# A LayerNorm-MLP mixer kernel: epsilon inside the statistics aggregation, a new order of loads, and a new order of steps

## The chip, the cores and the metric

The kernel runs on one core of a Trainium2 chip. The metric is device time in microseconds (us). A core has five engines that run side by side: TensorE (PE, matrix products), VectorE (DVE), ScalarE (ACT), GpSimd (POOL) and SyncE (SP), which here only issues DMAs. Engines wait for each other through semaphores.

## What is computed

```
B, S, D, F = 1, 2048, 512, 1792          # bfloat16
h  = gelu(layernorm(x) @ w1)
# four column blocks of h, shifted along S by 1, -1, 2, -2
g0 = shift(h[:, :, 0:128],  +1); g1 = shift(h[:, :, 128:256], -1)
g2 = shift(h[:, :, 256:384], +2); g3 = shift(h[:, :, 384:512], -2)
x1 = x + concat(g0, g1, g2, g3) @ w2
out = x1 + gelu(layernorm(x1) @ w3) @ w4
```

layernorm subtracts the mean over D and divides by sqrt(variance + 1e-5); there is no gain and no bias.

## The kernel before

The 2048 rows are 16 tiles of 128. Each tile passes through the two layers; q numbers the normalisations: q = t in layer 1 and q = 16 + t in layer 2. All of x, of the weights and of the intermediate results stays in SBUF.

For a tile, `ln(layer, t)` records the statistics and the normalisation. On DVE the statistics are bn_stats (L420) and bn_aggr (L422), which leave mean and variance in `mv`; then `vpe` (L427, on DVE or, by the table `VPE`, on POOL) adds epsilon, and POOL computes `rstd` (L438) as vpe to the power of -1/2. For the q in `STAT_ACT` the sums come from two ACT passes instead (L390 for the sum in layer 1, L395 for the squares), with three small DVE instructions behind them (L399 mean, L402, L406). The normalisation `norm` runs on DVE (L459), ACT (L468) or POOL (L471), by the table `NORM`; for the last two a small `nmr` (L464) goes ahead.

The normalised tile must be transposed to `xnT`. For seven tiles PE does it (the steps `sa`/`sb`, `ty`; L504, with the copy out of PSUM `ev` at L512 on the engine that `EVAC` gives). For the other 25 a DMA transpose issued by SP does it (`tp`, L477).

PE's steps stand in a list, `SCRIPT`, and PE runs them in that order: `warm` (L701, matmuls of zeros), `ra`/`rb` and `up1:0`, `up1:1` (tiles 0 and 1 in rows, L542, with gelu at L561 and a transpose `th` at L579, copied out at L585, `evh`), `up1:g` (group g of layer 1, L608, gelu at L623 to `hT`), `mix:t` (tile t times w2, L648, added to x by `x1` at L655 or L659), `up2:g` (group g of layer 2, L608, gelu at L623 to `h2T`), and `down:t` (L677, added and stored at L685 and L688). `GROUPS` says how many tiles each group has.

The loads stand in a second list, `LOADS`. `x7-8` is one DMA of two tiles, `w4a` is half of w4 (896 KB), `@act` puts a load on ACT's queue and all others go to SP. A `tp16` in this list holds a place: the loads behind it are issued only after that transpose has been issued. Names of tiles that PE transposes are skipped there.

All other order is made when the program is built. `order()` gives each instruction a latest start: it counts back from the PE steps through all edges, the edges of the load line among them. `place()` then runs a list schedule with rough durations and writes each engine's order; loads always go first as soon as their line allows it. On the chip each engine runs its own list in order.

```
LOADS = """
x0 w1a w1b x5 tp0 x4 x3 tp5 w2a w2b x7-8 x6 x1@act x11 w3 tp1 x14-15 tp16 x9 x13 x2@act x12 x10 w4b tp2 tp5
tp8 w4a
"""
```

Of the kernel before, what the change touches and what calls it, by code (L numbers as in the profile page):

```python
# [6 lines left out]
P = 128  # L7
ACT_F = mybir.ActivationFunctionType
ALU = mybir.AluOpType
# [16 lines left out]
class Program:  # L26
# [5 lines left out]
    DUE = 191823.0  # L32
    BEGIN = {"sp": 30.0, "act": 150.0, "pe": 400.0, "dve": 150.0, "pool": 450.0}
    ENTRY = 1900.0
    LAG = {"load": 150, "tp": 700}
# [114 lines left out]
    def place(self, succs, order_only):  # L150
# [9 lines left out]
        clock = moved = self.total = 0.0  # L160
# [35 lines left out]
        def land(op):  # L196
            nonlocal moved
            if op.queue == "tp":
                at = max(clock + 500.0, op.start + 2450.0) + self.LAG["tp"]
            elif op.name.startswith("out"):  # L200
                at = clock + 300.0
                self.total = max(self.total, at)
            else:
                moved += op.dur
                at = clock + 650.0 + min(450.0, 0.25 * moved) + (1200.0 if op.dur > 1400.0 else 0.0) + self.LAG["load"]
            for j in succs[op.idx]:
                if (op.idx, j) not in order_only:
                    release(op, self.ops[j], at + 30.0)

        while len(out) < len(self.ops):  # L210
# [18 lines left out]
            if op.queue:  # L229
                tp = op.queue == "tp"  # L230
                free[e] = start + (1300.0 if tp else 460.0)
                rings[e].append([start + (1400.0 if tp else 1000.0), 600.0 if tp else op.dur, op])
                for j in succs[op.idx]:
                    if (op.idx, j) in order_only:
                        release(op, self.ops[j], None)
            else:
                free[e] = start + op.dur
                for j in succs[op.idx]:
                    o = self.ops[j]
                    hop = self.HOP[e] if o.eng != e else (0.0 if e == "pe" else 120.0)  # L240
                    release(op, o, None if (op.idx, j) in order_only else start + op.dur + hop)
# [5 lines left out]
GROUPS = {1: (1, 1, 1, 1, 1, 1, 2, 4, 2, 1, 1), 2: (2, 2, 4, 4, 4)}  # L247
NORM = {5: "pool", 8: "pool", 9: "pool", 10: "act", 11: "pool", 13: "act", 15: "pool", 22: "pool", 23: "act", 26: "pool", 27: "act", 29: "act", 30: "pool"}
EVAC = {2: "dve", 4: "dve", 6: "both", 8: "both", 9: "dve", 10: "both", 11: "both", 13: "dve", 14: "dve", 16: "dve", 17: "both", 18: "dve", 19: "dve", 20: "both", 21: "both", 23: "both", 24: "dve", 25: "dve", 26: "dve", 27: "dve", 28: "dve", 29: "both", 30: "dve"}
SQRT = ()  # L250
STAT_ACT = (1, 7, 8, 11, 18, 19, 20, 21, 25, 26, 27, 28)
HALF = ()
TAIL = (256, 128, 128)
VPE = {0: "pool", 1: "pool", 2: "pool", 3: "pool", 6: "pool", 7: "pool", 8: "pool", 9: "pool", 12: "pool", 14: "pool", 15: "pool", 17: "pool", 19: "pool", 21: "pool", 24: "pool", 25: "pool", 26: "pool", 28: "pool", 29: "pool", 30: "pool", 31: "pool"}
NMR = {0: "pool", 1: "pool", 3: "pool", 4: "pool", 5: "pool", 6: "pool", 8: "pool", 11: "pool", 12: "pool", 13: "pool", 18: "pool", 19: "pool", 20: "pool", 22: "pool", 24: "pool", 26: "pool", 27: "pool"}
NAT = (0, 1)
SPLIT = (0,)
HEV = {3: "dve", 6: "dve"}
BIAS = {"bnag14": -1183, "bnag2": 166.078, "bnag9": -1516, "bnst18": -801.25, "nmr19": 740, "nmr7": 262.923, "nmr9": 377, "norm21": 198.168, "norm31": 61, "ssq0": -1049, "ssq14": -444, "sum17": -602, "tp19": 63, "tp9": 722.116, "vpe7": -589, "vpe8": 45, "x1_3": -682}
LOADS = """  # L260
x0 w1a w1b x5 tp0 x4 x3 tp5 w2a w2b x7-8 x6 x1@act x11 w3 tp1 x14-15 tp16 x9 x13 x2@act x12 x10 w4b tp2 tp5
tp8 w4a
"""
SCRIPT = """
warm:8 sa:0 sb:0 ty:1 ra:0 rb:0 up1:1 th:0 ty:2 th:1 up1:2 mix:0 ty:3 mix:1 ty:4 up1:3 ty:5 up1:4 mix:2
up1:5 mix:3 ty:17 mix:4 up2:0 up1:6 up2:1 mix:6 mix:5 up1:7 down:3 mix:9 up1:8 mix:7-8 up1:9 mix:10-11
up1:10 mix:13 down:0 mix:14 up2:2 down:1 mix:15 up2:3 mix:12 down:7 down:2 down:5 down:11 down:6 up2:4
down:9 down:4 down:8 down:13 down:10 down:12 down:14-15
"""

def bass_standalone__mixer_s_mlp__prompt_kernel(nc, x, w1, w2, w3, w4, out):
# [14 lines left out]
    with ExitStack() as es:  # L286
# [13 lines left out]
        st6 = sb("st6", [P, 2 * NT, 6], F32)  # L300
# [4 lines left out]
        sdv = sb("sdv", [P, 2 * NT], F32)  # L305
        sums = sb("sums", [P, 2 * NT, 2], F32)
        st6b = sb("st6b", [P, len(HALF) + 1, 2, 6], F32)
# [30 lines left out]
        def consts():  # L338
# [5 lines left out]
                   reads=[(("ident",), 0)], writes=[(("ident",), 1)], dur=300)  # L344
            pg.add("pool", "epsc", lambda e: e.memset(eps_c[:], LN_EPS), writes=[(("eps",), 0)], dur=70)
# [6 lines left out]
        def load(item):  # L352
            name, _, eng = item.partition("@")
            eng = eng or "sp"
            if name[0] == "x":
                a, _, b = name[1:].partition("-")
                t0, t1 = int(a), int(b or a) + 1
                if t0 in HALF:
                    for hh, e2 in ((0, "sp"), (1, "act")):
                        cs = slice(hh * D // 2, (hh + 1) * D // 2)  # L360
                        yield pg.add(e2, f"dma_x{t0}_{hh}",
                                     (lambda c: (lambda e: e.dma_start(x_sb[:, t0, c], xt[:, t0, c])))(cs),
                                     writes=[(("x", t0, hh), 0)], dur=190.0, queue=e2)
                else:
                    yield pg.add(eng, f"dma_x{t0}",
                                 lambda e: e.dma_start(x_sb[:, t0:t1, :], xt[:, t0:t1, :]),
                                 writes=[(("x", t, hh), 0) for t in range(t0, t1) for hh in (0, 1)],
                                 dur=(t1 - t0) * 430.0, queue=eng)
            else:
# [7 lines left out]
                             dur=(c1 - c0) * P * src.shape[1] * 2 / (300.0 if src.shape[1] == D else 380.0), queue=eng)  # L377
# [3 lines left out]
        def ln(layer, t):  # L381
            q = t if layer == 1 else NT + t
            src = x_sb[:, t, :] if layer == 1 else x1_sb[:, t, :]
            rs = [(("x", t, 0), 0), (("x", t, 1), 0)] if layer == 1 else [(("x1", t), 0)]
            col = lambda a: a[:, q : q + 1]
            if q in STAT_ACT:
                if layer == 1:
                    b, v = next_junk()
                    pg.add("act", f"sum{q}",
                           (lambda d: (lambda e: e.activation(d, src, ACT_F.Copy, accum_out=sums[:, q, 0:1])))(  # L390
                               junk[:, b, :]),
                           reads=rs, writes=[(("sum", q), 0), (("junk", b), v)], dur=610)
# [5 lines left out]
                pg.add("dve", f"mean{q}",  # L398
                       lambda e: e.tensor_scalar(mv[:, q, 0:1], sums[:, q, 0:1], 1.0 / D, None, ALU.mult),  # L399
                       reads=[(("sum", q), 0)], writes=[(("mv", q), 0)], dur=75)  # L400
# [8 lines left out]
            else:  # L409
                if layer == 1 and t in HALF:  # L410
                    k = HALF.index(t)
                    for hh in (0, 1):
                        pg.add("dve", f"bnst{q}_{hh}",
                               (lambda hh: (lambda e: e.bn_stats(st6b[:, k, hh, :],
                                                                 src[:, hh * D // 2 : (hh + 1) * D // 2])))(hh),
                               reads=[rs[hh]], writes=[(("st6", q, hh), 0)], dur=335)
                    pg.add("dve", f"bnag{q}", lambda e: e.bn_aggr(mv[:, q, :], st6b[:, k, :, :]),
                           reads=[(("st6", q, 0), 0), (("st6", q, 1), 0)], writes=[(("mv", q), 0)], dur=90)
                else:
                    pg.add("dve", f"bnst{q}", lambda e: e.bn_stats(st6[:, q, :], src),  # L420
                           reads=rs, writes=[(("st6", q), 0)], dur=605)
                    pg.add("dve", f"bnag{q}", lambda e: e.bn_aggr(mv[:, q, :], st6[:, q, :]),  # L422
                           reads=[(("st6", q), 0)], writes=[(("mv", q), 0)], dur=75)
                if q not in SQRT:
                    eng = VPE.get(q, "dve")
                    pg.add(eng, f"vpe{q}",
                           lambda e: e.tensor_scalar(col(vpe), mv[:, q, 1:2], LN_EPS, None, ALU.add),  # L427
                           reads=[(("mv", q), 0)], writes=[(("vpe", q), 0)], dur=70 if eng == "dve" else 240)
            if q in SQRT:
                assert q not in STAT_ACT  # L430
                pg.add("act", f"sqrt{q}",
                       lambda e: e.activation(col(sdv), mv[:, q, 1:2], ACT_F.Sqrt, bias=eps_c[:], scale=1.0),
                       reads=[(("mv", q), 0), (("eps",), 0), (("warm",), 0)], writes=[(("sdv", q), 0)], dur=190)
                pg.add("dve", f"rcp{q}", lambda e: e.reciprocal(col(rstd), col(sdv)),
                       reads=[(("sdv", q), 0)], writes=[(("rstd", q), 0)], dur=75)
            else:
                pg.add("pool", f"rstd{q}",
                       lambda e: e.tensor_tensor(col(rstd), col(vpe), neghalf[:], ALU.pow),  # L438
# [416 lines left out]
```

## Time and profile before

| what | value |
|---|---|
| median of 8 runs | 137.28 us (136.88 to 140.02) |
| the profiled execution | 137.3 us, span 136.0 us |
| PE busy | 131.9 us (97% of the span) |
| ACT, DVE, POOL busy | 56.7, 53.0, 29.5 us |
| granted TensorE clock | 1.00 |
| bytes read and written in HBM | 6.82 and 2.10 MB |

The span is the time between the first and the last recorded instruction; the remaining 1.3 us lie around it. In the lines of the profile, "L608" is a line of the kernel file, "y_ps<-xnT,w_sb" says which buffers an instruction writes and reads, "x72" counts merged instructions, and times are us from the start of the span. A line of waits reads: who waited, for whom, us in total, times, longest. A line of the timeline reads: start, duration, engine, line, operation. "DMA to landing" is the time from a DMA's issue to the arrival of its last byte.

### The profile page before, as it was taken

Reading aid. Unit: us, or ns where it says so; the run is one execution under the profiler, and the core shown is the slowest. Engines: PE = TensorE matmul, PEld = TensorE weight load, DVE = VectorE, ACT = ScalarE, POOL = GpSimd, SP = SyncE. Lnnn points to the kernel's source line nnn. Section 1 sums busy time; section 2 is a strip of 40 time slices with the busy share of each in tenths; the row PEclk is TensorE's granted clock in tenths of the full one; section 3 lists DMA queues with packets and bytes.
Section 4 is the critical chain, followed back from the end, with each engine's and each line's share of the span. In section 5 each row is a group of like instructions: output and inputs, shape, how many; then the busy total and the mean of one; then the engine's idle time right before and its main releaser. Section 6 shows DMA issues by size and latency. Waiting matters only on the chain.

```text
span 136.0 us, 2039 instructions
## 1 busy us (share of the span) xinstructions
PE 131.9 (97%) x792; PEld 71.4 (53%) x792; DVE 53.0 (39%) x155; ACT 56.7 (42%) x88; POOL 29.5 (22%) x70
## 2 busy tenths in 40 slices
PE   8999999699999999999999999999999999999994
PEld 3468687687446654444444444444444444444463
DVE  3879989850715796400061003323200002232222
ACT  6589966676433372655406665000055540000000
POOL 2636449990230119500002001000000000000000
DMA  6999589999622003451011000311110001111112
GB/s 210 321 366 389 79 226 268 167 290 119 128 52 64 5 0 77 89 104 39 5 39 38 0 0 0 77 39 43 39 39 0 0 0 39 39 43 39 39 39 77
DMA packets 21913, 12.32 MB, mean 91 GB/s; under 512 B 14480, under 2 KB 21392, under 8 KB 21904
## 3 DMA queue, kind: packets, MB, share of 16 engines
q1 hardware_dynamic: 21184, 11.80, 35.7%
q10 hardware_dynamic: 720, 0.39, 1.0%
q8 instruction: 6, 0.10, 0.3%
q14 instruction: 3, 0.02, 0.1%
HBM read 6.82 MB, written 2.10 MB: 66 GB/s over the span
## 4 chain that ended last, share of the span: by engine, by line
PE 91%; DMA 4%; DVE 2%; ACT 1%; POOL 0%; issue 0%; POOLq 0%; ACTq 0%
PE y_ps L608 40%; PE o_ps L677 36%; PE o_ps L648 10%; DMA xnT<-xn_buf 4%; PE o_ps L701 3%; PE y_ps L542 2%; PE y_ps L504 1%; ACT hn L561 1%; DVE xn_buf L459 0%; DVE x_sb L655 0%; POOL rstd L438 0%; PE o_ps L579 0%; DVE o_sb L685 0%; DVE xnT L512 0%; DVE mv L402 0%
## 5 line engine op out<-in xcount | busy, mean ns | idle before, releaser
L608 PE MATMUL y_ps<-xnT,w_sb 128*128 128x512 bf16 (+2 forms) x424 | 62.9, 307 | 1.3 <-DMA xnT<-xn_buf 1.3
L608 PEld LDWEIGHTS y_ps<-xnT,w_sb 128*128 128x128 bf16 x424 | 37.7, 98 | 26.2 <-ACT h2T L623 1.6
L677 PE MATMUL o_ps<-w_sb,h2T 128*128 128x512 bf16 (+2 forms) x252 | 49.2, 355 | 0.0
L623 ACT ACTIVATE h2T<-y_ps 128x1024 bf16<-128x1024 f32 (+1 forms) x29 | 28.6, 994 | 37.6 <-PE y_ps L608 37.6
L677 PEld LDWEIGHTS o_ps<-w_sb,h2T 128*128 128x128 bf16 x252 | 23.5, 98 | 25.2
L685 DVE TENSOR_TENSOR o_sb<-o_ps,x_sb 128x512 bf16<-128x512 f32 (+2 forms) x18 | 11.4, 632 | 55.5 <-PE o_ps L677 55.5
L438 POOL TENSOR_TENSOR rstd<-vpe,neghalf 128x1 f32<-128x1 f32 x32 | 17.9, 566 | 32.1 <-DVE vpe L406 21.8
L648 PE MATMUL o_ps<-w_sb,hT 128*128 128x512 bf16 x64 | 15.9, 379 | 0.0
L420 DVE BATCH_NORM_STATS2 st<-x_sb 128x6 f32<-128x512 bf16 x20 | 13.6, 681 | 2.3 <-DMA x_sb<-in_x_dram 2.1
L395 ACT ACTIVATE junk<-x_sb 128x512 bf16<-128x512 bf16 x12 | 7.5, 624 | 7.0 <-DVE x_sb L655 7.0
L623 ACT ACTIVATE hT<-y_ps 128x512 bf16<-128x512 f32 (+1 forms) x10 | 7.7, 766 | 4.6 <-PE y_ps L608 4.6
L655 DVE SCALAR_TENSOR_TENSOR x_sb<-o_ps,x_sb 128x512 bf16<-128x512 f32 x8 | 5.5, 686 | 10.4 <-PE o_ps L648 10.3
L459 DVE TENSOR_SCALAR xn_buf<-x_sb,mv,rstd 128x512 bf16<-128x512 bf16 x17 | 7.7, 457 | 4.3 <-POOL rstd L438 4.1
L648 PEld LDWEIGHTS o_ps<-w_sb,hT 128*128 128x128 bf16 x64 | 6.0, 98 | 5.5
L427 POOL TENSOR_SCALAR vpe<-mv 128x1 f32<-128x1 f32 x13 | 3.0, 245 | 21.5 <-DVE mv L422 20.3
L659 DVE TENSOR_TENSOR x_sb<-o_ps,x_sb 128x512 bf16<-128x512 f32 x8 | 5.5, 684 | 4.5 <-PE o_ps L648 4.5
L471 POOL TENSOR_SCALAR xn_buf<-x_sb,rstd,nmr 128x512 bf16<-128x512 bf16 x8 | 6.1, 766 | 0.6 <-DVE nmr L464 0.4
L468 ACT ACTIVATE xn_buf<-x_sb,nmr,rstd 128x512 bf16<-128x512 bf16 x5 | 4.0, 808 | 2.3 <-POOL nmr L464 2.0
L701 PE MATMUL o_ps<-zeros 128*128 128x512 bf16 x8 | 3.6, 631 | 0.6 <-POOLq L840 0.6
L422 DVE BATCH_NORM_AGGREGATE mv<-st 128x2 f32<-128x6 f32 x20 | 3.6, 178 | 0.4
L504 PEld LDWEIGHTS y_ps<-ident,xn_buf 128*128 128x128 bf16 x28 | 2.4, 113 | 1.3 <-DVE mv L399 0.3
L512 ACT ACTIVATE xnT<-y_ps 128x256 bf16<-128x256 bf16 (+1 forms) x6 | 2.8, 485 | 0.5 <-PE y_ps L504 0.5
(34 smaller groups left out, 32.4 us busy)
## 6 DMA issues: line engine op xcount, KB each, us to landing
out_dram<-o_sb SPq DMA_DIRECT2D x15, 128.0 KB, 1.7
w_sb<-in_w_dram SPq DMA_DIRECT2D x1, 1792.0 KB, 9.0
w_sb<-in_w_dram SPq DMA_DIRECT2D x2, 896.0 KB, 5.6
x_sb<-in_x_dram SPq DMA_DIRECT2D x10, 128.0 KB, 3.3
w_sb<-in_w_dram SPq DMA_DIRECT2D x4, 256.0 KB, 4.1
x_sb<-in_x_dram SPq DMA_DIRECT2D x2, 256.0 KB, 6.9
xnT<-xn_buf SPq DMA_TRANSPOSE x25, 2.5
x_sb<-in_x_dram ACTq DMA_DIRECT2D x2, 128.0 KB, 2.9
```

The costliest lines, as they stand in the source:

```text
L395: (lambda d: (lambda e: e.activation(d, src, ACT_F.Square, accum_out=sums[:, q, 1:2])))(junk[:, b, :]),
L420: pg.add("dve", f"bnst{q}", lambda e: e.bn_stats(st6[:, q, :], src), reads=rs, writes=[(("st6", q), 0)], dur=605)
L438: lambda e: e.tensor_tensor(col(rstd), col(vpe), neghalf[:], ALU.pow),
L459: lambda e: e.tensor_scalar(dst, src, mv[:, q, 0:1], rstd[:, q : q + 1], ALU.subtract, ALU.mult),
L471: f = lambda e: e.tensor_scalar(dst, src, rstd[:, q : q + 1], nmr[:, q : q + 1], ALU.mult, ALU.add)
L608: ins = e.matmul(y_ps[:, p, W * i : W * (i + 1)], wsb[:, dc, P * fc : P * (fc + 1)], src[:, dc, P * t0 : P * t0 + W], start=(dc == 0), sto ...
L623: (lambda d, s: (lambda e: e.activation(d, s, ACT_F.Gelu_apprx_tanh)))(dst, ysrc),
L648: ins = e.matmul(dst, hT[:, j, c0 : c0 + P], w2_sb[:, j, :], start=(j == 0), stop=(j == DC - 1))
L655: f = lambda e: e.scalar_tensor_tensor(x1_sb[:, t, :], dst, 1.0, x_sb[:, t, :], ALU.mult, ALU.add, accum_out=sums[:, NT + t, 0:1])
L677: ins = e.matmul(dst, h2T[:, fc, P * t : P * (t + 1)], w4_sb[:, fc, cs], start=(fc == 0), stop=(fc == FC - 1))
L685: (lambda d, c: (lambda e: e.tensor_tensor(o_sb[:, oi, c], d, x1_sb[:, t, c], ALU.add)))(dst, cs),
L701: ins = e.matmul(o_ps[:, b, :], zeros[:, 0:P], zeros[:], start=True, stop=True)
```

## The change

Epsilon: the statistics buffer has nine numbers for each tile instead of six. The last three are a third triple (0, 0, 512 x epsilon), set once by two memsets on POOL. bn_aggr over all three triples gives a variance that already holds epsilon, so `vpe` goes for the tiles whose statistics DVE computes. In layer 1 the ACT pass scales its sum by 1/512 and writes the mean itself. Branches that no tile used (`SQRT`, `HALF`) go.

Loads: the list begins with one run of loads without a transpose between them. w3 comes in halves. w4a and x10 stand behind tp16, w4b behind tp11, and x12-14 and x15 behind tp9.

Order: the rough durations in `place()` are changed (a transpose lands no sooner than 600 ns after the last load, the first PE steps are taken slower, a load behind another DMA costs 800 ns), and the tables and the script are new. `BIAS`, which shifted single instructions, is empty.

```
-            pg.add("dve", f"bnst{q}", lambda e: e.bn_stats(st6[:, q, :], src), ...)
-            pg.add("dve", f"bnag{q}", lambda e: e.bn_aggr(mv[:, q, :], st6[:, q, :]), ...)
-            if q not in SQRT:
-                eng = VPE.get(q, "dve")
-                pg.add(eng, f"vpe{q}", lambda e: e.tensor_scalar(col(vpe), mv[:, q, 1:2], LN_EPS, None, ALU.add), ...)
+            pg.add("dve", f"bnst{q}", lambda e: e.bn_stats(st9[:, q, 0:6], src), ...)
+            pg.add("dve", f"bnag{q}", lambda e: e.bn_aggr(mv[:, q, :], st9[:, q, :]), ...)
+        var = vpe[:, q : q + 1] if q in STAT_ACT else mv[:, q, 1:2]
...
+            pg.add("pool", "trip0", lambda e: e.memset(st9[:, :, 6:8], 0.0), ...)
+            pg.add("pool", "trip1", lambda e: e.memset(st9[:, :, 8:9], D * LN_EPS), ...)
...
-                           ... e.activation(d, src, ACT_F.Copy, accum_out=sums[:, q, 0:1])
+                           ... e.activation(d, src, ACT_F.Copy, scale=1.0 / D, accum_out=mv[:, q, 0:1])
...
-                at = max(clock + 500.0, op.start + 2450.0) + self.LAG["tp"]
+                at = max(clock + 500.0, op.start + 2450.0, last + 600.0) + self.LAG["tp"]
...
-GROUPS = {1: (1, 1, 1, 1, 1, 1, 2, 4, 2, 1, 1), 2: (2, 2, 4, 4, 4)}
-NORM = {5: "pool", 8: "pool", 9: "pool", 10: "act", 11: "pool", 13: "act", 15: "pool", 22: "pool", 23: "act", 26: "pool", 27: "act", 29: "act", 30: "pool"}
-EVAC = {2: "dve", 4: "dve", 6: "both", 8: "both", 9: "dve", ... 17: "both", ...}
-STAT_ACT = (1, 7, 8, 11, 18, 19, 20, 21, 25, 26, 27, 28)
+GROUPS = {1: (1, 1, 1, 1, 1, 1, 2, 2, 2, 2, 2), 2: (2, 2, 4, 4, 4)}
+NORM = {4: "act", 5: "act", 6: "act", 10: "act", 11: "pool", 12: "pool", 13: "act", 15: "act", 18: "pool", 20: "pool", 21: "pool", 22: "pool", 24: "act", 28: "act", 30: "pool"}
+EVAC = {1: "both", 2: "dve", 3: "dve", 7: "both", 9: "dve", ... 17: "both", ...}
+STAT_ACT = (1, 6, 8, 9, 12, 21, 22, 23, 27, 28, 29)
-HEV = {3: "dve", 6: "dve"}
-BIAS = {"bnag14": -1183, "bnag2": 166.078, "bnag9": -1516, ...}
+HEV = {2: "dve", 5: "dve", 6: "dve"}
+BIAS = {}
 LOADS = """
-x0 w1a w1b x5 tp0 x4 x3 tp5 w2a w2b x7-8 x6 x1@act x11 w3 tp1 x14-15 tp16 x9 x13 x2@act x12 x10 w4b tp2 tp5
-tp8 w4a
+x0 w1a w1b x4-5 w2b tp2 x3 w2a x6-7 w3b x8 w3a x1@act x9 x2@act x11 tp16 w4a x10 tp11 w4b tp9 x12-14 x15
 """
 SCRIPT = """
-warm:8 sa:0 sb:0 ty:1 ra:0 rb:0 up1:1 th:0 ty:2 th:1 up1:2 mix:0 ty:3 mix:1 ty:4 up1:3 ty:5 up1:4 mix:2
-up1:5 mix:3 ty:17 mix:4 up2:0 up1:6 up2:1 mix:6 mix:5 up1:7 down:3 mix:9 up1:8 mix:7-8 up1:9 mix:10-11
-up1:10 mix:13 down:0 mix:14 up2:2 down:1 mix:15 up2:3 mix:12 down:7 down:2 down:5 down:11 down:6 up2:4
-down:9 down:4 down:8 down:13 down:10 down:12 down:14-15
+warm:8 sa:0 sb:0 ty:1 ra:0 rb:0 up1:1 ty:2 th:0-1 up1:2 mix:0 ty:4 ty:3 mix:1 up1:3 ty:5 up1:4 mix:2 up1:5
+mix:3 ty:17 mix:4 up2:0 up1:6 up2:1 mix:6 down:1 mix:5 up1:7-8 mix:8 mix:7 up1:9 mix:10 down:0 down:2 mix:9
+up1:10 mix:12 mix:11 up2:2 mix:13 down:3 down:6 mix:14 up2:3 mix:15 down:4-5 down:7 down:11 down:9-10 up2:4
+down:8 down:12 down:14 down:13 down:15
 """
```

## The prediction

> **What bounds the kernel now.** I read the page first, rows 1, 2 and 4, then what PE waits for, then the chain in the window of the one real wait, then SP's order of issue and each transfer's time from issue to landing.
>
> ```profile
> PE 131.9 (97%) x792; PEld 71.4 (53%) x792; DVE 53.0 (39%) x155; ACT 56.7 (42%) x88; POOL 29.5 (22%) x70
> ...
> PE 91%; DMA 4%; DVE 2%; ACT 1%; POOL 0%; issue 0%; POOLq 0%; ACTq 0%
> ...
> PE y_ps L608 <- DMA xnT<-xn_buf: 1.3, 1, 1.3
> PE o_ps L701 <- POOLq L840: 0.6, 1, 0.6
> PE o_ps L579 <- ACT hn L561: 0.2, 1, 0.2
> ```
>
> PE is busy 97% of 136.0 us, and the chain that ended last is PE for 91%. The three lines of waits are everything that PE waits for. So a change can win only these waits, and can lose by opening new ones. The 0.6 is the entry. The 1.3 is one matmul group waiting for a DMA transpose:
>
> ```profile
> 18.75 0.59 POOL rstd L438 x2
> 19.34 5.46 DMA xnT<-xn_buf
> 24.79 0.14 issue
> 24.93 8.02 PE y_ps L608 x72
> ```
>
> The transpose was issued at 19.34 and landed 5.46 us later. SP's timeline around it:
>
> ```profile
> 17.09 0.43 SPq L366 DMA_DIRECT2D x_sb<-in_x_dram  x1
> 17.57 0.43 SPq L374 DMA_DIRECT2D w_sb<-in_w_dram  x1
> 18.05 6.51 SPq L477 DMA_TRANSPOSE xnT<-xn_buf  x5
> 24.60 0.58 SPq L374 DMA_DIRECT2D w_sb<-in_w_dram  x1
> ```
>
> The 17.57 load is w4b (896 KB), directly ahead of the transposes of tiles 6 and 7 that up1:6 needs. Asked one by one, w4b takes 5.4 us to landing (22.97); the first two transposes behind it take 6.3 and 5.5 (24.35 and 24.84). The last fourteen transposes, with no load ahead, take
>
> ```profile
> DMA to landing us min/median/max: 2.4/2.5/2.9
> ```
>
> So a transpose behind a load lands 1.4 to 1.9 us after that load. w4a (issued 24.60, landed 30.5) shows it again: the next transpose lands at 32.4. So does tp16: issued 13.61 behind x14-15 (landed 15.22), it lands at 17.21, 2.0 later.
>
> What the wait costs: up2:0 begins at 17.31 and is 56 matmuls of 256 columns. A group of 16 takes 1.75 in the chain, so 56 take 6.1 and up1:6 could begin at 23.4. It begins at 24.93, so 1.5 us are lost (the page's 1.3 counts from the modelled end).
>
> **The change part by part.**
>
> *PE work.* The script holds the same steps: 8 warm matmuls, seven PE transposes, 64 mix, 252 down and 424 up matmuls. One group of four tiles (3.45) becomes two of two (2 x 1.75); two single tiles (2 x 0.89) become one of two (1.75). +0.05 and -0.03: zero. The tail (down15 in 256, 128, 128) is unchanged.
>
> *Epsilon.* vpe goes from 20 tiles: 13 POOL instructions of 245 ns and 7 DVE of 152 ns. rstd follows bn_aggr directly, which shortens such a tile's chain by 0.2 to 0.3 us. Four means (144 ns of DVE) go as well. The two memsets are like the 98 ns ones on POOL and lie ahead of 3.05, the first bn_aggr: hidden, with over 1 us to spare. bn_aggr over nine numbers instead of six has no row; between 0 and half of its 178 ns more, I take 20 ns, hidden. None of these is on PE's chain except through a transpose that is late anyway for its load. Worth zero alone. If the cover goes (a tile that is just in time), it is worth its 0.25 us.
>
> *Engines of norms and statistics.* norm4, norm5, norm6 go to ACT (808 ns each, L468); ev3 leaves ACT, ev4 comes (592 each); half of ev1 goes to DVE. ACT was busy 8.16 of 8.70 us between 8.6 and 17.3, and DVE 8.17, but on ACT six statistics passes of 0.82 (0.63 and a 0.19 read) fill gaps there and can wait. What must run on ACT between 8.05 and 17.3 afterwards: evh0 and evh1 1.2, norm4 and norm5 1.6, four gelu 2.4, ev4 and ev5 1.2, half of ev17 0.4: 6.8 of 9.2 us. The tight place is norm4: ACT is free at 9.24, norm4 ends at 10.05, ty4 wants it at 10.25; gelu of up1:2 then ends at 10.65 and mix1 wants it at 10.70. Cost 0 to 0.8 (a statistics pass in the way); I take 0.1.
>
> *th0 and ty2 swapped.* th1 still waits for gelur1, which waits for the rows of tile 1. Zero.
>
> *Load order.* The first stream on SP becomes x0 w1a w1b x4-5 w2b x3 w2a x6-7 w3b x8 w3a x9 x11: thirteen issues, as before, of 0.4 to 0.5 us. With x1 and x2 on ACT that is 4,224 KB against 4,352. Before, 4,352 KB had landed at 15.22, and w3 moved 1,792 KB in 5.4 us, so 128 KB are 0.4: the stream lands at about 14.8. x4-5 lands near 6.0 as x4 did; x3 goes from 6.28 to about 7.0, and bnst, bnag, rstd and norm (0.7, 0.2, 0.6, 0.4) put it ready near 9.5 with DVE's queue, for ty3 at 10.5; both halves of w2 near 7.7, as before; w3a by 14.4, needed at 17.3. tp16 then lands at 14.8 + 2.0 = 16.8 against its need at 17.31.
>
> Behind tp16, SP issues w4a and x10. Before, x9 landed 0.5 after tp16, and w4b took 3.4 from the landing ahead of it to its own. So w4a lands near 20.5 and x10 near 21.0. tp6 and tp7 were issued at 18.05 and 19.34; if so again, they land at 22.4 and 22.9, needed at 23.4: the wait goes. Next late are tp18 and tp19 (23.3 and 24.0 by the spacing seen behind w4b, needed at 25.1). w4b now stands behind tp11, and down:1 stands at 32.1 (23.4 + 1.75 + 6.1 + 0.86), where the first down stood at 38.0. w4a in the old place took 5.9 from issue to landing, so w4b must be issued by 26.2. tp9 and x12-14 follow; up1:9, which needs 12 and 13, comes at 41.2, about 7 us after x12-14 can have landed (34).
>
> [...] The rows: alone, a transpose lands in 2.5, as an x load in the same stretch does (2.2 to 2.8); behind w4b it lands 1.4 after it, where x loads landed 0.4 to 0.8 apart, 0.6 in the mean. [...]
>
> *Sum.* 137.3 (the profiled execution: span 136.0 and 1.3 around it; the median of the runs is 137.28) - 1.5 for the wait + 0.1 for norm4 + 0.2 for new small waits on landings (each estimate of a landing is good to about 0.5, and two have that much slack) = **136.1**.
>
> **The rivals.**
>
> *A. The order does what it says* (136.1; own range 135.6 to 136.9). For it: every deadline above has 0.5 us or more. Against: 0.5 is little, and ACT's order is fixed beforehand.
>
> *B. down:1 waits for w4b: slower.* The place is PE after mix6, at 32.1. w4b can't be issued before norm11 has run, and x11 is the last tile of the first stream. Before, nothing hung on tile 11 until 34.5, and the transposes of tiles wanted then went out at 25.2 to 30.7. If tp11 goes out at 28.1, as the third behind w4a did, w4b is issued at 29.4 and lands at 35.3: PE waits 3.2, and the time is 136.1 + 3.2 = 139.3. It decides from an issue of about 27.8 on, where the wait eats the 1.5. Against: the due times pass through the edges of the load line, so norm11 is due from down:1 (about 25), not from up1:8. The opposite fault has the same price: tp11 out before tp18 and tp19 puts w4b's 3.4 us ahead of them, and up2:1 waits about 3 us at 25.1.
>
> *C. The load moves, the wait stays: same.* w4a and x10 still lie ahead of tp6 and tp7. If tp16 goes out at 15 instead of 13.6, or the loads behind it are held, x10 lands at 22.5 to 23 and tp7 at 24.4 to 24.9: up1:6 waits 1.0 to 1.5 again, 137.1 to 137.6. Against: tile 16's chain lost its 0.25 us of vpe.
>
> *D. ACT is overfull* with three more norms before 17.3: two or three waits of 0.4 to 0.8, 137 to 138.
>
> **How the numbers follow.** A measurement of this kernel tells about 0.2% (0.27 us) from no change. A 0.58: nearly all faster. B 0.20: slower. C 0.12: half same, a third slower, the rest faster. D 0.10: half slower, the rest between. That gives faster 0.61, same 0.10, slower 0.29. The range 135.6 to 138.4 holds A, C, D and the mild third of B; what it leaves out is most of B and little below.
>
> **What would show it.** Right: PE's waits lose "PE y_ps L608 <- DMA xnT<-xn_buf" or show it under 0.5; no L427 and no L399 for layer 1; tp16 lands before 17.3, tp6 and tp7 before 23.4; w4b is issued before 26.2. Wrong: "PE o_ps L677 <- DMA w_sb" (B), the L608 wait at the same place (C), PE waiting for ACT between 9 and 17 (D), or PE's busy time off 131.9 by over 0.3.

## The result and the profile after

The kernel after takes 135.56 us in the median of 11 runs (135.25 to 136.12), the kernel before 137.28 in the median of 32. The ratio is 0.9879, 95% interval 0.9856 to 0.9902: faster by 1.2%. Ratios, here and below, are to the kernel before timed beside the run, and leave out executions that took over 1.5% more than the fastest of their kernel. The forecast was 136.1 with a range from 135.6 to 138.4; the median lies 0.04 under the lower end, within the rounding of that end.

The page of the kernel after, its busy row and its chain, and then everything that PE waits for:

```profile
PE 130.8 (98%) x792; PEld 72.6 (54%) x792; DVE 52.0 (39%) x140; ACT 58.4 (44%) x90; POOL 25.8 (19%) x59
...
PE 97%; ACT 1%; issue 0%; DVE 0%; POOLq 0%; ACTq 0%
...
PE o_ps L679 <- POOLq L815: 0.6, 1, 0.6
PE o_ps L557 <- ACT hn L539: 0.4, 1, 0.4
PE y_ps L520 <- ACT xnT L490: 0.2, 1, 0.2
```

DMA has left the chain (4% before), and no matmul waits for a DMA transpose any more. (up, L608 before, is L586 now; the DMA transposes, L477, are L455; the rows of tiles 0 and 1, L542, are L520; L557 is the transpose `th`.) The small waits at L520 and L557 lie ahead of up1:2 and are for ACT. In the chain in order of time the place of the old wait reads:

```profile
16.09 0.86 PE o_ps L626 x4
16.95 13.97 PE y_ps L586 x128
30.93 0.86 PE o_ps L626 x4
```

up2:0, up1:6 and up2:1 are 56, 16 and 56 matmuls: 128 in one piece. Before, they were 56, a gap, and 72. SP's timeline behind the first stream of loads, and the time to landing of the first transpose of the row of five:

```profile
13.46 1.61 SPq L455 DMA_TRANSPOSE xnT<-xn_buf  x1
15.12 0.58 SPq L372 DMA_DIRECT2D w_sb<-in_w_dram  x1
15.75 0.56 SPq L365 DMA_DIRECT2D x_sb<-in_x_dram  x1
17.25 6.59 SPq L455 DMA_TRANSPOSE xnT<-xn_buf  x5
...
DMA to landing us min/median/max: 4.1/4.1/4.1
```

tp16, w4a, x10, then tp6, tp7, tp18, tp19 and tp11. tp6 lands at 21.35 and tp7 at 22.60, and up1:6 needs them at 22.9 (up2:0 starts at 16.79, and its 56 matmuls are 56 of 128 parts of the 13.98 to mix6). Landings in this text are an issue time plus a time to landing, good to 0.05. Only then comes w4b: issued at 23.89, landed at 29.99, needed by down:1 at 31.63.

The two profiled executions side by side, by stages of PE:

| stage | before, us | after, us |
|---|---|---|
| to the first PE transpose | 4.03 | 4.03 |
| to up1:2 (transposes, rows and th of tiles 0 and 1) | 4.46 | 3.93 |
| to up2:0 | 8.82 | 8.83 |
| up2:0, to the start of up1:6 | 7.62 | 6.11 |
| up1:6 and up2:1 | 7.85 | 7.87 |
| the rest | 103.22 | 103.13 |
| span | 136.0 | 133.9 |

Of 2.1 us, 1.51 is the wait at up1:6. Another 0.53 lies before up1:2, where the change does nothing to PE's work but a swap of two transposes; the experiments show that executions of one kernel differ by more than that there. The medians differ by 1.7, not by 2.1.

### The profile page after: what moved, and what is told of

It is laid out like the page before. It is cut to its first block, busy times and chain, and to the rows that moved or that the text cites. A ratio compares the mean times of both kernels' runs of the same rounds, so it can differ in the third digit from the quotient of the medians.

```text
span 133.9 us, 2025 instructions
## 1 busy us (share of the span) xinstructions
PE 130.8 (98%) x792; PEld 72.6 (54%) x792; DVE 52.0 (39%) x140; ACT 58.4 (44%) x90; POOL 25.8 (19%) x59
## 4 chain that ended last, share of the span: by engine, by line
PE 97%; ACT 1%; issue 0%; DVE 0%; POOLq 0%; ACTq 0%
PE y_ps L586 45%; PE o_ps L655 36%; PE o_ps L626 10%; PE o_ps L679 3%; PE y_ps L520 1%; PE y_ps L482 1%; ACT hn L539 1%; PE o_ps L557 0%; ACT xnT L490 0%; DVE o_sb L663 0%; POOLq L815 0%; ACTq L779 0%
## 5 line engine op out<-in xcount | busy, mean ns | idle before, releaser
L586 PE MATMUL y_ps<-xnT,w_sb 128*128 128x256 bf16 (+2 forms) x424 | 62.6, 307 | 0.0
L586 PEld LDWEIGHTS y_ps<-xnT,w_sb 128*128 128x128 bf16 x424 | 39.0, 98 | 23.4 <-DVE xnT L490 0.3
L601 ACT ACTIVATE h2T<-y_ps 128x1024 bf16<-128x1024 f32 (+1 forms) x29 | 28.6, 994 | 42.6 <-PE y_ps L586 42.6
L416 POOL TENSOR_TENSOR rstd<-mv,neghalf 128x1 f32<-128x1 f32 x21 | 11.6, 554 | 42.2 <-DVE mv L411 39.7
L637 DVE TENSOR_TENSOR x_sb<-o_ps,x_sb 128x512 bf16<-128x512 f32 x10 | 6.9, 686 | 12.7 <-PE o_ps L626 12.7
L633 DVE SCALAR_TENSOR_TENSOR x_sb<-o_ps,x_sb 128x512 bf16<-128x512 f32 x6 | 4.1, 690 | 16.8 <-PE o_ps L626 16.8
L601 ACT ACTIVATE hT<-y_ps 128x1024 bf16<-128x1024 f32 (+1 forms) x9 | 7.4, 827 | 6.3 <-PE y_ps L586 6.2
L416 POOL TENSOR_TENSOR rstd<-vpe,neghalf 128x1 f32<-128x1 f32 x11 | 6.0, 549 | 18.8 <-DVE vpe L405 18.7
L446 ACT ACTIVATE xn_buf<-x_sb,nmr,rstd 128x512 bf16<-128x512 bf16 x8 | 6.5, 812 | 4.9 <-DVE nmr L442 3.2
L393 ACT ACTIVATE junk<-x_sb 128x512 bf16<-128x512 bf16 x11 | 6.8, 622 | 2.7 <-DVE x_sb L633 2.7
L411 DVE BATCH_NORM_AGGREGATE mv<-st 128x2 f32<-128x9 f32 x21 | 4.0, 191 | 0.2
L388 ACT ACTIVATE junk<-x_sb 128x512 bf16<-128x512 bf16 x5 | 3.1, 623 | 0.2 <-DMA x_sb<-in_x_dram 0.2
```

What stands on the lines that cost most here:

```text
L393: (lambda d: (lambda e: e.activation(d, src, ACT_F.Square, accum_out=sums[:, q, 1:2])))(junk[:, b, :]),
L416: lambda e: e.tensor_tensor(col(rstd), var, neghalf[:], ALU.pow),
L446: f = lambda e: e.activation(dst, src, ACT_F.Identity, bias=nmr[:, q : q + 1], scale=rstd[:, q : q + 1])
L586: ins = e.matmul(y_ps[:, p, W * i : W * (i + 1)], wsb[:, dc, P * fc : P * (fc + 1)], src[:, dc, P * t0 : P * t0 + W], start=(dc == 0), sto ...
L601: (lambda d, s: (lambda e: e.activation(d, s, ACT_F.Gelu_apprx_tanh)))(dst, ysrc),
L637: f = lambda e: e.tensor_tensor(x1_sb[:, t, :], dst, x_sb[:, t, :], ALU.add)
```

## Experiments

The theory: the gain is the wait at up1:6, and it went because fewer loads lie ahead of the transposes of tiles 6 and 7. Rivals: the tables and the script made it, or the shorter statistics chain did.

### The load alone, put back and taken away

**w4b put back ahead of tp6 and tp7, in the kernel after.**

```
-... x11 tp16 w4a x10 tp11 w4b tp9 x12-14 x15
+... x11 tp16 w4a x10 w4b tp11 tp9 x12-14 x15
```

> The kernel after, with only tp11 and w4b exchanged in the load line, so that w4b again lies ahead of tp6 and tp7, now behind w4a and x10. Theory with the delay as traced: x10 lands at 20.9, w4b 3.4 later at 24.3, tp6 and tp7 1.4 to 1.9 after that, near 25.7 and 26.1; up1:6, due at 22.9, waits 3.2: about 138.8. If transposes behind a load were as quick as loads behind a load: tp7 near 25.5, wait 2.6, about 138.1. Rival (the load order is not what matters): 135.3 to 135.9.

The profiled execution took 138.35 us at a granted clock of 1.00 (the other three had 0.988; the median of the four is 140.01). PE's waits and the matmuls after the wait:

```profile
PE y_ps L586 <- ACT xn_buf L446: 2.3, 1, 2.3
...
26.00 8.02 PE L586 MATMUL y_ps<-xnT,w_sb 128*128 128x256 bf16 x72 [2.34 <-ACT xn_buf L446]
```

The wait is back at its old place, before the same 72 matmuls. The profile names ACT's norm as the releaser, but that had long been done: x10 lands at 21.4, w4b at 24.1, the first transpose at 25.35 and the second at 25.85, just before PE's 26.00. So the delays behind the load are 1.3 and 1.8, the landings forecast from the old trace (24.3, 25.7, 26.1) hold to 0.4, and two transposes spaced as the x loads of the old trace (0.6 in the mean) would by estimate have landed at 24.7 and 25.3. up1:6 was due at 17.38 + 6.1 = 23.5: 2.5 lost here, the rest of the 3.1 over the kernel after being the second half of w1, which landed late in this execution (PE waited 0.6 for it).

**w4b behind tp19 in the kernel before, every engine's order kept.**

```
         pg.order()
+        w4b = next(op for op in pg.seq if op.name == "dma_w4b")
+        pg.seq.remove(w4b)
+        pg.seq.insert(next(i for i, op in enumerate(pg.seq) if op.name == "tp19") + 1, w4b)
```

> The kernel before with every engine's order kept and one instruction moved: on SP, w4b goes from ahead of the transposes of tiles 6, 7, 18 and 19 to directly behind them. Theory: with x10 landing at 19.6 the four land near 20.5, 21.2, 22.5, 23.8; up1:6 starts at its due 23.4 and up2:1 and both mixes follow without a wait to about 33.0 (before: 34.5). Then the second delay shows: w4b and w4a land one after the other (w4a near 31.5), the transpose of tile 11 lands near 34 to 35 as before, and up1:7, which takes tiles 8 to 11 together, waits for it 1.0 to 2.0. Time 136.8 to 137.8: the wait moves and nothing is won. Rival (w4b's place alone is the whole gain): 135.7 to 136.1. Rival (w4b's place doesn't matter): up1:6 still waits over 1 us.

Ratio 1.0081 (1.0034 to 1.0127): nothing is won. The timelines of SP and of PE show where the wait went:

```profile
17.43 5.13 SPq L477 DMA_TRANSPOSE xnT<-xn_buf  x4
22.61 0.58 SPq L374 DMA_DIRECT2D w_sb<-in_w_dram  x1
23.24 1.25 SPq L477 DMA_TRANSPOSE xnT<-xn_buf  x1
24.53 0.58 SPq L374 DMA_DIRECT2D w_sb<-in_w_dram  x1
...
16.73 14.14 PE L608 MATMUL y_ps<-xnT,w_sb 128*128 128x256 bf16 x128
30.71 1.89 PE L648 MATMUL o_ps<-w_sb,hT 128*128 128x512 bf16 x8
35.04 5.19 PE L608 MATMUL y_ps<-xnT,w_sb 128*128 128x512 bf16 x16 [2.44 <-DMA xnT<-xn_buf]
```

The first wait is gone: the four transposes land at 20.0, 21.7, 22.5 and 23.8, and PE runs 128 matmuls in one piece, as in the kernel after. But the two halves of w4 now land one behind the other (28.6 and 33.0), the transposes of tiles 9 to 11 that follow land at 33.9 to 34.9, and up1:7, which takes tiles 8 to 11 at once, waits 2.44 for them. The old order had a second delay hidden under the first. And the wait costs more than its own length here: the 16 matmuls after it take 5.19 us, where the same 16 take 3.62 in the kernel before:

```profile
34.51 3.62 PE L608 MATMUL y_ps<-xnT,w_sb 128*128 128x512 bf16 x16
```

That belongs to this execution, one of seven of the twelve with a granted clock of 0.988; they took 139.2 to 139.6, the five at 1.00 137.2 to 138.3. The median is 139.23.

**The same wish written in the old load line and planned anew.**

```
-... x12 x10 w4b tp2 tp5 tp8 w4a
+... x12 x10 tp6 tp7 tp18 tp19 w4b tp8 tp9 tp10 tp11 w4a
```

> The kernel before, with only its load line edited: w4b stands behind the transposes of tiles 6, 7, 18 and 19, and w4a behind those of 8 to 11. Theory (the wait at up1:6 comes from w4b lying ahead of tp6 and tp7): both land near 20.5 to 22, 2.5 after issue; up1:6 starts without a wait near 23.4, and up2:1 follows. PE's line 'L608 <- DMA xnT<-xn_buf' loses its 1.3 at this place; a smaller new wait may come at up1:7 or down:3, since w4b and w4a land later (30 and 36). Time 135.8 to 136.6. Rival (the new order of steps and tables made the gain): no change beyond 0.3 us, 137.0 to 137.6.

140.43 us, ratio 1.0201 (1.0132 to 1.0269): a miss. At up1:6 it did what the theory says (transposes of tiles 6 and 7 landed at 19.6 and 20.6, 128 matmuls in one piece). But PE waited 2.8 for DVE at its transpose of tile 17 and 1.0 before up1:4. The due times pass through the load line, and the new plan put the work of tiles 6, 7 and 18 ahead of that of tile 17 on DVE. The run says nothing of what w4b's place is worth; the one with the order kept does.

### Loads against tables and script

**Old tables and script, new load line.** The edit is the LOADS line of the change, alone.

> The kernel before with the load line of the kernel after, planned anew by the old rules. Theory (512 KB fewer lie ahead of the transposes of tiles 6 and 7): no wait over 0.4 for a transpose at up1:6. But the old script takes tiles 8 to 11 as one group and 12 and 13 soon after, while x12 to x15 now come last, so a wait of 0 to 2 may come at up1:7 or up1:8. 135.8 to 137.5. Rival (tables and script make the gain): the wait at up1:6 stays, 137.0 to 138.5.

143.09 us, ratio 1.0469 (1.0389 to 1.0548): a miss, and mainly by one large wait. (All four executions had a granted clock of 0.976 or 0.988. In the profile the clock is 0.80 in the 7.6 us behind the wait, so the loss is more than the wait itself.)

```profile
PE y_ps L607 <- DMA xnT<-xn_buf: 4.4, 1, 4.4
...
18.39 5.31 SPq L476 DMA_TRANSPOSE xnT<-xn_buf  x4
23.75 0.58 SPq L373 DMA_DIRECT2D w_sb<-in_w_dram  x1
24.38 2.56 SPq L476 DMA_TRANSPOSE xnT<-xn_buf  x2
```

Four transposes go ahead of w4b, and one of them is tp11, since w4b hangs on it. So one of tiles 6, 7, 18 and 19 is left for after w4b, tile 19, and up2:1 wants it: PE runs 72 matmuls (up2:0 and up1:6), then stands 4.4 us until the transpose behind w4b has landed at 30.1. In the kernel after five go ahead of w4b.

**New tables and script, old load line.** The reverse edit in the kernel after.

> The kernel after with the load line of the kernel before. Theory: w4b again lies ahead of the transposes of tiles 6 and 7 behind four x tiles; they land near 24.4 and 24.9 and up1:6, due near 22.9, waits 1.5 to 2.1; 136.9 to 137.8. Rival (the tables and the script make the gain): 135.3 to 136.0.

137.12 us, ratio 1.0016 (0.9985 to 1.0047): all of the gain is lost. w4b lands at 22.4 and the two transposes at 23.0 and 24.3; up1:6 starts at 24.47. Only 0.6 of that shows as a wait for a DMA. PE had lost 0.7 before (up1:3 waited for the copy of tile 3), so it came late to a place where it would have had to wait anyway. The place of the wait fits the theory, its size was split.

So neither half carries the gain alone. The loads take the wait away, and the script and tables are what they need to fit.

### Epsilon

**The triple alone, in the kernel before.**

```
+            pg.add("pool", "trip0", lambda e: e.memset(st6[:, :, 6:8], 0.0), ...)
+            pg.add("pool", "trip1", lambda e: e.memset(st6[:, :, 8:9], D * LN_EPS), ...)
-                    pg.add(eng, f"vpe{q}", ...)
```

> The kernel before with the epsilon triple alone, loads and script as before. Theory: tp6 and tp7 still wait for w4b; 137.0 to 137.5, with the wait at up1:6 between 1.0 and 1.6. Rival (epsilon made the gain): 135.6 to 136.2, no wait at up1:6.

137.52 us, ratio 1.002 (0.9988 to 1.0052): nothing. w4b lands at 23.22, the two transposes at 24.50 and 25.04, up1:6 starts at 25.10. PE got there later (its rows took 2.69 us in this execution, 2.35 in that of the kernel before), and up1:6 still started within 0.2 of the old 24.93. The wait shown is so only 0.7, below the 1.0 to 1.6 expected: the load sets that time, and what is won or lost ahead of it doesn't count.

**The triple undone in the kernel after, planned anew, and then with the order kept.** The second edit puts each vpe back behind its bn_aggr on DVE, or ahead of its rstd on POOL, in the finished order:

```
-    lambda e: e.bn_aggr(mv[:, q, :], st9[:, q, :])
+    lambda e: e.bn_aggr(mv[:, q, :], st9[:, q, 0:6])
         pg.order()
+        # each bnag on DVE is followed by its vpe, or each rstd on POOL is led by it, by the old table VPE
```

> The kernel after with the epsilon triple undone: bn_aggr over six numbers and the vpe instruction back for 21 tiles, on the engines that the old table gives. Theory: off PE's chain, 135.4 to 135.9, with PE's waits as after (0.2 and 0.4); tp16 issues 0.2 to 0.3 later, near 13.7. Rival (the shorter statistics chain made the gain, or the planned order depends on it): 136.5 to 137.3 with a wait for a transpose of 1 us or more.

136.41 us, ratio 0.9943 (0.9911 to 0.9974). PE waited 0.5 and 0.2 before its transposes of tiles 4 and 3: the rival was nearer than the theory, though its one wait of 1 us or more did not come. Since the order had changed too, the second form:

> The kernel after with every engine's order kept, bn_aggr over six numbers, and a vpe instruction put back for each of the 21 tiles, behind bn_aggr on DVE (150 ns) or ahead of rstd on POOL (245 ns). Theory (the triple shortens chains that are just in time in the new order, as the run without it showed at the PE transposes of tiles 4 and 3): a wait of 0.2 to 0.6 in all before PE's transposes near 10; time 135.8 to 136.3. Rival (the 0.85 of the run without the triple came from its other planned order): 135.4 to 135.7, no new wait. Rival (epsilon is the gain): 136.8 or more.

136.22 us, ratio 0.9957 (0.9934 to 0.998). It was then run again, beside the kernel after:

> The kernel after with its order kept and the vpe instructions put back, timed beside the kernel after. If epsilon is worth what the first pair of separate runs gave, it is 0.6 to 1.1 us slower than the kernel after, 136.0 to 136.6. If that difference was the chip's, it is within 0.3 us.

> The kernel after, unchanged, timed on the same chip as the run without the triple in its order, so that the two can be compared directly. 135.3 to 135.8. If the time before up2:0 depends on when the clock rises and not on the kernel, the rows of tiles 0 and 1 take anything between 1.9 and 2.7 us in this profile too.

136.31 us against 135.47: the triple is worth 0.84 us in the new order, with twelve executions against six. The timeline of the first of the two runs shows a piece of it:

```profile
9.01 0.22 POOL L737 TENSOR_SCALAR vpe<-mv 128x1 f32<-128x1 f32 x1 [0.43 <-DVE mv L412]
9.31 0.57 POOL L417 TENSOR_TENSOR rstd<-vpe,neghalf 128x1 f32<-128x1 f32 x1
9.99 0.41 DVE L438 TENSOR_SCALAR xn_buf<-x_sb,mv,rstd 128x512 bf16<-128x512 bf16 x1 [0.49 <-POOL rstd L417]
10.46 0.40 PE L483 MATMUL y_ps<-ident,xn_buf 128*128 128x128 bf16 x4 [0.30 <-DVE xn_buf L438]
```

Tile 3: vpe on POOL, rstd behind it, then the norm on DVE, then PE's transpose 0.30 late. In the kernel after both transposes of this place run together at 9.77. The step behind them starts 0.48 later (10.69 against 10.21). From there to up2:0 the lag grows to 0.73 (17.52 against 16.79), by several starts of 0.1 or less, and no wait stands behind it any more that would swallow it. The second pair of profiles, first the kernel after, then vpe back, at the start of up1:2 and of up2:0:

```profile
7.98 1.06 PE L586 MATMUL y_ps<-xnT,w_sb 128*128 128x128 bf16 x16
16.81 14.14 PE L586 MATMUL y_ps<-xnT,w_sb 128*128 128x256 bf16 x128
...
8.69 1.06 PE L587 MATMUL y_ps<-xnT,w_sb 128*128 128x128 bf16 x16
18.15 14.15 PE L587 MATMUL y_ps<-xnT,w_sb 128*128 128x256 bf16 x128
```

From up1:2 to up2:0 it is 8.83 and 9.46: a lag of 0.63 in the same stage. up1:6 waits for no transpose in either, so the triple is not what took the old wait away. But without it the change wins 0.6, 0.8 and 1.1 us in the three runs with vpe back, against 1.7 and 1.8 with it.

### The slow first matmuls, and the warm matmuls

**Seven warm matmuls in place of eight, in the kernel after** (`warm:8` to `warm:7`).

> The kernel after with seven warm matmuls in place of eight, everything else as planned before. In the profile after, the eighth ends at 4.2 while the normalised half of tile 0 is ready near 3.6. If that is what holds the first transposes, they start 0.4 sooner, the rows of tile 0 start near 4.6 (the first half of w1 lands at 4.2, the second at 5.0), and everything to the end moves by 0.2 to 0.4: 135.1 to 135.4. Rival: w1b's landing near 5.0 or the later rise of the clock takes it back: 135.4 to 135.8.

135.81 us, ratio 0.9896 (0.9839 to 0.9952): no gain over the kernel after (135.56 and 135.47). The transposes started 0.23 sooner, but the rows of tiles 0 and 1 took 2.63 us in its profile. That row decides little, as the same order profiled twice shows (the kernel with vpe back, first and second run):

```profile
5.01 1.89 PE L521 MATMUL y_ps<-w_sb,xnT 128*128 128x512 bf16 x8
...
5.00 2.62 PE L521 MATMUL y_ps<-w_sb,xnT 128*128 128x512 bf16 x8
```

Over thirteen executions of old and new orders (the one with the late w1 left out) these eight matmuls took 1.89 to 1.94 seven times, and 2.08, 2.35, 2.37, 2.62, 2.63 and 2.69 otherwise: some still ran at a low rate, and how many differed between executions of one order (1.89 and 2.62 above). The granted clock reads 1.00 in this stretch of every profile, so only the durations show it: in the rows of the kernel before, such a matmul takes up to 631 ns (the eight warm ones take 607 to 634), as one does under a granted clock of 0.50 in the run with w4b behind tp19 (35.04 to 38.30), and 379 otherwise. What sets the number of such matmuls, no run here shows. Old orders gave 1.89 to 2.69 and new ones 1.89 to 2.63, so the 0.46 of this stage between the two profiles (2.35 and 1.89) lies within the draw of one execution and can't be credited to the change.

### What a transpose waits for

**w4b issued by ACT instead of SP, in the kernel after**, behind the first gelu of up2:0.

```
+        w4b.eng = "act"
+        pg.seq.insert(next(i for i, op in enumerate(pg.seq) if op.name == "gelu2_0_4"), w4b)
```

> The kernel after with w4b issued by ACT (behind the first gelu of up2:0, near 19.8) instead of by SP behind tp11; all other order kept. It asks whether a transpose waits for every load in flight or only for those ahead of it on its own queue. Own queue: the transposes of tiles 18, 19 and 11 (issued 19.8 to 22.6) land 2.5 to 3.5 after issue, near 23.2, 23.8 and 25.1 as now, though w4b is still moving until about 24; time 135.3 to 135.8. Every load in flight: they land 1 or more after w4b, near 25 to 26, and up2:1, due at 24.6, waits 0.5 to 1.5: 136.0 to 137.2.

140.73 us, ratio 1.0232 (1.0156 to 1.0309), at granted clocks of 0.976 and 0.988: slower than either forecast. PE's wait, ACT's issue of w4b, its time to landing, and that of the transpose which SP had issued at 18.69, before it:

```profile
PE y_ps L586 <- DMA xnT<-xn_buf: 4.0, 1, 4.0
...
18.94 0.40 ACTq L372 DMA_DIRECT2D w_sb<-in_w_dram  x1
...
DMA to landing us min/median/max: 8.2/8.2/8.2
...
DMA to landing us min/median/max: 8.4/8.4/8.4
```

w4b and the transpose of tile 7 both land at 27.1, though the transpose was issued first and on another queue (it landed at 22.6 in the kernel after); those of 18 and 19 land at 27.3 and 27.8. w4b itself takes 8.2 against 6.1, but here w4a and x10 were still in flight until 20.9. So in this run a load on the other queue held the transposes up too, and that queue was no way around it. Whether they wait for the load or share the transfer time with it is not shown.

## Why the prediction was right, and where it was off

**The sum.** 136.1 forecast, 135.56 measured. 0.3 of the difference is the two terms below that measured 0; the other 0.2 is not located, and is less than the draw of the rows at the start.

**The wait.** Right in place and size: 1.5 forecast, 1.51 in the stage table. The landings: first stream 14.1 (14.8 forecast), tp16 16.2 (16.8), w4a 20.4 (20.5), x10 20.85 (21.0), tp6 21.35 (22.4), tp7 22.6 (22.9), tp18 and tp19 23.2 and 23.8 (23.3 and 24.0). The delay of 1.4 to 1.9 behind a load was good for the second transpose (1.8 to 1.9 in three runs) and too long for the first (0.5 here, 0.6 behind w4b with the old load line, 1.3 with w4b put back). tp19 came right for another reason: it was issued at 21.1 and landed 2.7 later, near the 2.5 of a transpose alone. SP issues one transpose in 1.3 us (the row of five takes 6.59), and that pace set its landing, not a spacing behind the load.

**Two spacings.** For the transposes behind w4b two rows of the old trace gave two estimates: the delay of 1.4 to 1.9 after a load, and the 0.6 from one x load to the next, which puts two transposes 0.6 and 1.2 after it. With w4b put back they came 1.3 and 1.8 after it. So the delay was the better for the second transpose, which is the one that ends the wait. It is no fixed delay: the first transpose came 0.5 and 0.6 after the load in two of the three runs above, and with the new load line in the old kernel the two behind w4b came 0.5 and 1.2 after it (29.6, then 30.1 and 30.7), as the spacing of the x loads has it. What decides between them stays open.

**The new waits, +0.2, and norm4, +0.1.** Both terms were too large: they measured 0. No landing was late, and ty4 ran at 9.77 directly behind mix0. norm4 could start at 8.66 rather than 9.24, since the rows were done 0.5 earlier in this execution.

**Epsilon, "worth zero alone".** The term that was mis-sized. Alone in the old order it is zero, as said. In the new order it is 0.84: the norms of tiles 3 and 4 are just in time there, and nothing later swallows a lag. The prediction named this case (a tile just in time, 0.25) and did not price it over the several tiles in a row that it meets. The small terms were right: bn_aggr takes 13 ns more (20 forecast), and the memsets 170 and 160 ns (98 forecast), still hidden.

**Two sizes that cancel.** From up1:2 to up2:0 PE takes 8.82 us in the kernel before, 9.55 and 9.46 in the new order with vpe back, and 8.83 in the kernel after. So the new loads, tables and script lengthen this stage by 0.6 to 0.7, and the triple takes that back. The prediction had 0.1 (norm4) for the first and 0 for the second. That the sum held is in this part luck: 136.1 is near what the new order takes with vpe back (136.2 to 136.4), not what it takes with the triple. Which of the new parts lengthens the stage was not separated.

**Rival B** stayed away: tp11 went out at 22.57 and w4b at 23.89, 2.3 before the limit of 26.2. Its opposite fault, tp11 ahead of a transpose that up2:1 needs, is what the old tables made of the new load line: a wait of 4.4 where about 3 was forecast. **C** and **D** did not come.

**The sign that failed.** PE's busy time was to stay within 0.3 of 131.9, and is 130.8. 0.9 of the 1.1 lies between 4.03 and up1:2, before and after:

```profile
4.03:8.49 4.46, 4.22 (x30) 2.30 (x28) 3.18 (x11) 2.95 (x6) 1.57 (x4) 1.00 1.08 336
...
4.03:7.96 3.93, 3.31 (x29) 2.04 (x28) 3.15 (x10) 2.59 (x6) 1.27 (x3) 1.00 1.05 355
```

(The columns are the stretch, its length, busy time and count of PE, PEld (its weight loads), DVE, ACT and POOL, the granted clock, the DMA share and GB/s.) PE is busy 4.22 and 3.31 us with nearly the same matmuls (30 and 29): a matmul at the low rate is longer busy, in the rows up to 631 ns against 379. The sign took equal work for equal busy time, and the rate was not equal.

## What to carry to other kernels

When PE is busy 97% of the time, list its few waits and ask of each what is next late; in the old order, moving one load took the first wait away and uncovered a second that cost more. A cost that is hidden behind a wait comes to light when the wait goes, so price small edits in the new order, not in the old one. And when the order is planned by a program, test one edit with the order kept: two of the edits that were planned anew lost 3 and 6 us to waits other than the one that they were to test.

## What the runs showed of the hardware

- DMA transposes were held up behind a load on SP's queue (6.3 and 5.5 us to landing behind w4b in the kernel before, 2.5 with no load ahead), and one of them beside a load on ACT's queue that was issued after it (8.4 us with w4b there, 4.1 in the kernel after; one profile each).
- In the run with w4b behind tp19, a wait of PE of 2.4 us was followed by 3.3 us at a granted clock of 0.50 (35.04 to 38.30). The window after the wait has a granted clock of 0.68 (columns as above):

```profile
35.04:40.10 5.06, 5.06 (x17) 1.95 (x18) 0.41 (x1) 1.02 (x1) 1.62 (x3) 0.68 0.53 104
```

16 matmuls took 5.19 instead of 3.62: the wait of 2.4 became a loss of 4.0. With w4b put back it did not come: the 7.85 us behind a wait of 2.3 have a granted clock of 1.00.
- bn_aggr over nine numbers took 191 ns in the mean (kernel after), over six 178 (kernel before).
